# An attention-plus-wave-mixer kernel whose static order is planned anew: mixer weights earlier, batch 1 by head pair, two-chunk evictions, new issue times

## The chip, the cores and the metric

The kernel runs on one core of a Trainium2 chip. The metric is device time in microseconds (us), the median of several executions. Executions of one kernel mostly agree within a per cent; a few fall in a slower state, told by a time over 1.5% above the fastest of the same kernel. Wherever I give a ratio, it is the mean time of one kernel's fast runs over that of the other kernel's fast runs of the same rounds, so it is not quite the ratio of the medians that stand beside it, which count the slow runs too.

The engines: PE is TensorE (PEld its weight loads), DVE is VectorE, ACT is ScalarE, POOL is GpSimd, SP is SyncE, which here does nothing but issue DMAs. In these traces each engine works off its own instructions in the emitted order: further down, VectorE stands idle for 2.82 us before a cast while work behind it has its data. That is what this case is about.

## The reference, cut to what matters

Eight batches, eight heads, 576 positions, head size 64. Linear attention (q times the 64x64 matrix k-transposed v), a root-mean-square norm, then a mixer over 512 channels:

```python
kv = np.einsum('bhsd,bhse->bhde', k, v)
out = np.einsum('bhsd,bhde->bhse', q, kv)
x = out / np.sqrt(np.mean(out * out, -1, keepdims=True) + 1e-6) * g_norm   # then heads side by side: [b, 576, 512]
theta = x @ w_theta
zr, zi = x * np.cos(theta), x * np.sin(theta)
y = einsum('ts,bsd->btd', w_tok_r, zr) + einsum('ts,bsd->btd', w_tok_i, zi)
u = x + y
return u + np.maximum(u @ w_ch, 0)
```

## The kernel before

The source does not fix the order of the instructions. It registers tasks (a load, a cast, a group of matmuls), each with an estimated cost on the engines that may do it, a due time, and what it needs. A planner, run when the kernel is built, simulates engines and DMA with these estimates and emits each task when its simulated turn comes. The emitted order is final: on the chip, an engine whose next instruction lacks its data stands still, even when a later instruction could run.

The planner's picture of the DMA is a single server. Of its loop (cuts marked by ...):

```python
RATE = 0.335e6          # bytes per us
BACKLOG = 3.5
...
if dma is not None:
    (first, size, packed) = dma
    begin = max(start + first, dma_free)
    dma_free = begin + size / self.RATE / packed
    end = dma_free + 0.35
done[name] = end
```

The q of batches 2 and later is cast to f16 on VectorE and turned by five transposing DMAs:

```python
nc.sync.dma_start_transpose(
    out=st["qT", b][:, :, j * P:j * P + rows],
    in_=qcast[b % 2][:rows, j].rearrange("p h d -> p (h d)"),
)
weave.add(("qT", b, j), [SP], due("turn_q", b, j), fn, ..., dma=dma(128e3, 0.24))
```

The last 64 rows of each batch are stored in two issues (`parts` are two halves of the partitions):

```python
for (half, r) in parts:
    nc.sync.dma_start(out=out[b, SF:S, r * n:(r + 1) * n], in_=t[half])
```

The token mix makes one matrix y per chunk of 128 channels and half of the positions, evicted as `uT = y * gcol + xT` by VectorE. At the start, "warm" matmuls on unused data fill TensorE's time.

## Time and profile before

The time before was 231.53 us (231.21 to 233.05); the profiled span is 230.3 us.

| | before |
|---|---|
| useful TensorE work, at the spacing of undisturbed stretches | about 194 us |
| first token-mix product y of batch 0 starts | 44.3 us |
| mixer weights issued | 23 to 33 us |
| last y products end, span ends | 222.2, 230.3 us |

Three views of the kernel before follow. First, from the page: the busy tenths of TensorE in 40 slices of the span, the granted clock of TensorE in tenths, the busy share of the DMA engines, and the chain of work that ended last.

```profile
PE   7999999999996999999999999999999999999992
PEclk9999999999999999999999999999999999999999
DMA  5899999999749996974899467996894412103214
PE 73%; DMA 9%; DVE 6%; ACT 5%; POOL 3%; issue 1%; SPq 1%; DVEq 0%
```

TensorE is busy from slice 1 to the end with one dip near 70 us, and three quarters of the chain is TensorE. DMA fills the first half of the span and thins out after three quarters.

Second, the median time from issue to landing of the large loads (tile, queue, kind and count, size, us).

```profile
q<-in_q_dram SPq DMA_DIRECT2D x32, 256.0 KB, 5.1
k<-in_k_dram SPq DMA_DIRECT2D x28, 256.0 KB, 5.1
v<-in_v_dram SPq DMA_DIRECT2D x28, 256.0 KB, 5.5
```

### The profile page before, as it was taken

The page shows a single profiled execution, that of the slowest core. Times are in us where ns is not written, and L with a number is a line of the kernel's source. Part 1 is how long each engine was busy: PE and PEld are TensorE (multiplying, and loading weights), DVE is VectorE, ACT ScalarE, POOL GpSimd, SP SyncE. Part 2 cuts the span into 40 slices and gives each one's busy share as a digit, 9 for nine tenths or more (in the row PEclk, how much of TensorE's full clock was granted, in tenths as well). Part 3 has the DMA queues.
Part 4 walks back from the last instruction along what each step waited for, and adds up shares of the span by engine and source line. Part 5 has one row for each costly group of instructions (what it writes and reads, how often), then busy time and mean ns, then how long its engine had stood idle before and what let it go on. Part 6 is the DMA issues. An engine that isn't in the chain of part 4 may idle for free.

```text
span 230.3 us, 5955 instructions
## 1 busy us (share of the span) xinstructions
PE 220.8 (96%) x2342; PEld 145.8 (63%) x2342; DVE 185.2 (80%) x368; ACT 157.3 (68%) x298; POOL 88.0 (38%) x108
## 2 busy tenths in 40 slices
PE   7999999999996999999999999999999999999992
PEld 2674555786754665677667766865675668655861
DVE  2268599279997798799999997998799989987553
ACT  2477687327995688767896877589849797877031
POOL 8000197436513670464266033543275336430000
PEclk9999999999999999999999999999999999999999
DMA  5899999999749996974899467996894412103214
GB/s 184 291 344 239 291 254 313 330 272 335 127 124 260 340 162 159 331 235 82 190 317 353 90 151 213 318 195 155 234 306 122 117 57 93 48 23 137 71 46 159
DMA packets 59931, 46.42 MB, mean 202 GB/s; under 512 B 29056, under 2 KB 52608, under 8 KB 59904
## 3 DMA queue, kind: packets, MB, share of 16 engines
q1 hardware_dynamic: 59840, 46.05, 71.9%
q8 instruction: 18, 0.29, 0.6%
q14 instruction: 9, 0.07, 0.1%
q0 software_dynamic: 64, 0.00, 0.0%
HBM read 33.06 MB, written 9.44 MB: 185 GB/s over the span
## 4 chain that ended last, share of the span: by engine, by line
PE 73%; DMA 9%; DVE 6%; ACT 5%; POOL 3%; issue 1%; SPq 1%; DVEq 0%
PE y L893 27%; PE vps L937 11%; PE th L806 11%; PE kv L524 6%; DMA wst<-in_moe_w_theta_dram 4%; PE xTps L775 4%; PE ups L928 4%; PE warm L293 3%; DMA vl<-in_v_dram 3%; PE raw L572 3%; DMA v<-in_v_dram 2%; POOL rt L594 2%; ACT tr L849 2%; DVE x L606 2%; PE wTps L432 2%; PE th L811 1%
## 5 line engine op out<-in xcount | busy, mean ns | idle before, releaser
L893 PE MATMUL y<-wT,z 128*128 128x320 f16 (+1 forms) x576 | 79.1, 286 | 2.2 <-DVE z L859 2.2
L893 PEld LDWEIGHTS <-z 128*128 128x128 f16 x576 | 54.0, 98 | 19.1 <-DVE z L859 2.8
L594 POOL TENSOR_TENSOR rt<-ss,mhalf 128x8 f32<-128x8 f32 x35 | 61.0, 1744 | 2.9
L590 POOL TENSOR_SCALAR ss<-ss 128x8 f32<-128x8 f32 x35 | 9.5, 271 | 85.2 <-DVE ss L583 84.6
L901 DVE SCALAR_TENSOR_TENSOR uT<-y,gcol,xT 128x256 f16<-128x256 f32 (+1 forms) x64 | 32.7, 512 | 7.9 <-PE y L893 7.6
L937 PE MATMUL vps<-wch,uT 128*128 128x512 f16 (+1 forms) x192 | 37.7, 344 | 0.0
L818 ACT ACTIVATE pt<-th,magic_t 128x512 f32<-128x512 f32 (+1 forms) x40 | 25.7, 642 | 16.6 <-PE th L806 13.3
L806 PE MATMUL th<-wth,xT 128*128 128x512 f16 x128 | 32.7, 380 | 0.0
L784 ACT ACTIVATE xT<-xTps,gcol 128x512 f16<-128x512 f16 (+1 forms) x36 | 22.9, 635 | 13.3 <-PE xTps L775 13.0
L944 ACT COPY u<-ups 128x512 f16<-128x512 f16 (+1 forms) x40 | 21.0, 537 | 14.9 <-PE ups L928 14.6
L859 DVE TENSOR_TENSOR z<-x,tr 128x1024 f16<-128x1024 f16 (+1 forms) x40 | 27.0, 674 | 3.4 <-ACT tr L849 1.7
L948 DVE SCALAR_TENSOR_TENSOR ot<-vps,u 128x512 f32<-128x512 f32 (+1 forms) x40 | 25.2, 633 | 4.1 <-PE vps L937 2.6
L822 DVE SCALAR_TENSOR_TENSOR f<-pt,th 128x512 f32<-128x512 f32 (+1 forms) x40 | 25.2, 629 | 4.0 <-ACT pt L818 3.7
L606 DVE TENSOR_TENSOR x<-raw,rt 128x512 f16<-128x512 f32 x36 | 24.7, 685 | 3.0 <-POOL rt L594 2.4
L583 DVE TENSOR_REDUCE ss<-sq 128x8 f32<-128x512 f32 x36 | 24.3, 680 | 2.3 <-ACT sq L579 2.0
L293 PE MATMUL warm<-kvbd 128*128 128x512 f16 x81 | 23.4, 410 | 2.0 <-DVE pio_t L250 1.5
L841 ACT ACTIVATE tr<-fa,pio_t 128x512 f16<-128x512 f32 x32 | 23.0, 720 | 0.5 <-DVE fa L829 0.3
L841 ACT ACTIVATE tr<-f 128x512 f16<-128x512 f32 x32 | 20.2, 630 | 3.4 <-DVE f L822 3.2
L579 ACT ACTIVATE sq<-raw 128x512 f32<-128x512 f32 x36 | 21.1, 591 | 1.2 <-PE raw L572 0.9
L937 PEld LDWEIGHTS <-uT 128*128 128x128 f16 (+1 forms) x192 | 14.1, 102 | 8.1 <-issue 0.4
L524 PE MATMUL kv<-v,k 128*64 128x64 f32 x448 | 19.0, 227 | 0.0
L524 PEld LDWEIGHTS kv<-v,k 128*64 128x64 f32 x448 | 15.3, 137 | 5.6 <-issue 4.2
(80 smaller groups left out, 243.4 us busy)
## 6 DMA issues: line engine op xcount, KB each, us to landing
q<-in_q_dram SPq DMA_DIRECT2D x32, 256.0 KB, 5.1
out_dram<-ot SPq DMA_DIRECT2D x32, 256.0 KB, 3.6
k<-in_k_dram SPq DMA_DIRECT2D x28, 256.0 KB, 5.1
v<-in_v_dram SPq DMA_DIRECT2D x28, 256.0 KB, 5.5
k<-in_k_dram SPq DMA_DIRECT2D x4, 288.0 KB, 6.2
v<-in_v_dram SPq DMA_DIRECT2D x4, 288.0 KB, 6.4
wmix<-in_moe_w_tok_r_dram SPq DMA_DIRECT2D x4, 288.0 KB, 5.5
wmix<-in_moe_w_tok_i_dram SPq DMA_DIRECT2D x4, 288.0 KB, 4.0
```

Of the source, the lines that this page charges most:

```text
L293: nc.tensor.matmul(t[:], kv_bd[1][:, 0, :], kv_bd[1][:].rearrange("p h c -> p (h c)"), start=True, stop=True,)
L524: nc.tensor.matmul(kvp[r * D:(r + 1) * D, hp, :], st["k", b, hp][:, r, j, :] if j < NF else st["kl", b][:, 2 * hp + r, :], st["v", b, hp][ ...
L594: nc.gpsimd.tensor_tensor(out=r[:], in0=t[:], in1=mhalf[:], op=ALU.pow)
L606: nc.vector.tensor_tensor(out=t[:].rearrange("p (h e) -> p h e", h=H), in0=st[raw][:].rearrange("p (h e) -> p h e", h=H), in1=st[rt][:].un ...
L806: nc.tensor.matmul(t[:], xT[:, kc, :], wth[:, kc, :], start=(kc == 0), stop=(kc == NK - 1),)
L818: nc.scalar.activation(out=t[:], in_=st[th][:], func=AFT.Identity, bias=magic_t[:])
L822: nc.vector.scalar_tensor_tensor(out=t[:], in0=st[pt][:], scalar=MAGIC, in1=st[th][:], op0=ALU.subtract, op1=ALU.subtract,)
L841: nc.scalar.activation(out=t[:, which, :], in_=src[:], func=AFT.Sin, scale=-RAD, bias=0.0 if bias is None else bias[:],)
L859: nc.vector.tensor_tensor(out=t[:], in0=xb.unsqueeze(1).broadcast_to((P, w, C)), in1=st[tr][:, 0:w, :], op=ALU.mult,)
L893: nc.tensor.matmul(t[:], z[:, kc * P:(kc + 1) * P], wT[m][:, cols], start=(m == 0), stop=(m == NM - 1),)
L901: nc.vector.scalar_tensor_tensor(out=st["uT", b][:, kc, cols], in0=st[y][:], scalar=gcol[:], in1=st["xT", b][:, kc, cols], op0=ALU.mult, o ...
L937: nc.tensor.matmul(t[half], uT(kc), wch[:, kc, r * n:(r + 1) * n], start=(kc == 0), stop=(kc == NK - 1),)
```

## The change

Its intent: shorten the start (get to y earlier), take some work off VectorE, and plan the order with a finer picture of SyncE, on which an issue now takes 0.4 to 1.3 us, where it took 0.1 before. Its core, with cuts; the due times, period, margins and the `MIX_AFTER`/`WCH_AFTER` places of the weights were all searched anew:

```diff
-    "load": (-15.33, 2.93),       # due times of the tasks, 17 entries
+    "load": (-20.73, 4.16),       # 21 entries, all changed
 ...
-MIX_AFTER = 5
-WCH_AFTER = 7
+MIX_AFTER = 3                     # mixer weights before batch 1's loads
+WCH_AFTER = 6
-    RATE = 0.335e6
-    BACKLOG = 3.5
+    LANES = 8
 ...
-                dma_free = begin + size / self.RATE / packed
-                end = dma_free + 0.35
+                dma_free = max(start + first, dma_free) + took
+                end = dma_free + 0.2
 ...
-    SP = ("SP", 0.1, 0.1)
+    def sp(cost):
+        return ("SP", cost, cost, False)
 ...                                # loads of 256 KB: 0.78 us before
-                      makes=[(kind, f"{kind}{b}_{hp}")], dma=dma(size, 1.0), load=True)
+                      makes=[(kind, f"{kind}{b}_{hp}")], dma=dma(0.71), load=True)
 ...                                # transposing DMAs of q
-            weave.add(("qT", b, j), [SP], ..., dma=dma(128e3, 0.24))
+            weave.add(("qT", b, j), [sp(1.3)], ..., dma=dma(0.5))
 ...                                # g_norm as a row, turned by a matmul with sqrt(D)
-                nc.gpsimd.dma_start(out=gcol[r * D:(r + 1) * D, :], in_=g_norm.unsqueeze(1))
+                nc.gpsimd.dma_start(out=grow[:, r * D:(r + 1) * D], in_=g_norm.unsqueeze(0))
 ...                                # batch 1 goes through the head-pair path of batch 0
-            if b == 0:
-                first(hp)
-                continue
-            if b == 1:
-                turn_q_by_pe(b, hp)
-            attention(b, hp)
+            if b < 2:
+                by_pair(b, hp)
+            else:
+                attention(b, hp)
 ...                                # mix: half 0 in banks of two chunks
-        (half, kc) = divmod(i, NK)
+        half = int(i >= NK // 2)
+        kcs = [i - NK // 2] if half else [2 * i, 2 * i + 1]
 ...                                # last 64 rows of a batch in one store
-            for (half, r) in parts:
-                nc.sync.dma_start(out=out[b, SF:S, r * n:(r + 1) * n], in_=t[half])
+            nc.sync.dma_start(
+                out=out[b, SF:S, :].rearrange("t (r c) -> r t c", r=len(parts)), in_=t[:]
+            )
```

In batch 0 half 0's sums are also left open, so that y accumulates as the z tiles appear; and the casts of the weights may go to VectorE and ScalarE as well as GpSimd.

## The prediction

> **What bounds it now.** The page gives PE busy 220.8 of 230.3 us, but 81 matmuls of that are idle work ("warm"): start to start in the timeline they cover 21.5 us, before 45 us. Useful matmuls (as many after) at their usual spacing (0.216 us per 128x512, 0.136 per 128x320, 0.109 per 128x256, 0.73 per 20 kv) sum to about 194 us. So PE is the limit from 44 us on (chain of waits: mostly y, vps, th); the start is what can be saved. There the timeline shows: theta begins at 25.2 us; mixer weights are issued only from 23 us, after two head pairs of batch 1; GpSimd casts them from 28.2 to 38.6; the last turned wT is kept near 43.9; the first y starts at 44.3 although the last z of batch 0 ended at 39.3. Another 3 us go at 68.7 to 71.9: y of batch 1 waits for DVE z.
>
> **What the change does.**
> - Mixer loads move straight behind theta (program order): 1.8 MB of batch 1 no longer precede them, 6 us at the page's 300 GB/s. DVE and ACT share the casts.
> - Half 0 of batch 0's mix accumulates as z tiles appear, and batch 1's attention goes by head pair: PE has real work while it waits (54 warm instead of 81).
> - Half 0 evictions: 32 of 128x256 (477 ns, 0.4 spacing) become 16 of 512 columns (about 0.6): 3 us less DVE in all, little each; DVE is not the later limit (about 20.5 us per batch against 22-23 on PE).
> - The Sin table load (1.28 us; the Trainium skill, "ScalarE: Activation LUTs", What ACT_TABLE_LOAD costs, has 1283 ns) sits at 22.05 before the last xT of batch 0; moved behind: theta 1 us earlier.
> - g_norm: gcol is ready at 13.7 now, first used at 14.6: worth nothing.
> - Last store in one issue: -0.5 us.
>
> **Cost.** At the start DVE now limits. From the first f (about 26.3 us) its new order up to batch 0's last uT adds up, at measured spacings, to 24.4 us: done at about 51 instead of 62. In the order, 163.5 us of useful PE work remain from batch 0's last y product, which then starts near 49.5. Add 3 to 6 us of stalls (3 us after 96 us in this trace) and 4.4 us of tail: 220.5 to 223.5 us span; the reported time was 1.2 us above the span. DVE or ACT, in order, may stand behind a late cast: up to 2 us more. GpSimd casts beside z stretched it to 1.0-1.3 us (mean 0.74) at 30-38 us, as the Trainium skill's "SBUF — State Buffer", Who interferes with whom, says for tensor_tensor with two SBUF inputs; casts now end by about 30.
>
> **Predicted:** 222.8 us, 8 in 10 between 219 and 228. Faster by over 2%: 0.87; within 2%: 0.11; slower: 0.02.
>
> **What would show it.** Right: mixer DMAs issued from 13-20 us; casts over by 31; first y about 35, last uT of batch 0 near 51; first y of batch 1 near 64 (now 68.4, really 71.9), no DVE z wait; batch spacing unchanged at about 23 us.
>
> **What would make it wrong.** DVE or ACT stalled on late casts; batch 1's later loads starving its head pairs; "mm" banks held longer by two-chunk y, so PE waits for evictions; the serial pow on GpSimd (1.7 us, five for batch 1) delaying batch 1's x.

## More of the kernel before

Third, the waits of VectorE for q (total us, times, longest).

```profile
DVE qcast L453 <- DMA q<-in_q_dram: 4.9, 2, 2.7
DVE qcast L459 <- DMA ql<-in_q_dram: 1.9, 1, 1.9
```

They are few, and all three lie in the first 26 us. The order of this kernel fits the arrival of its data.

## The result, and the profile after

The changed kernel took **249.2 us** (246.45 to 250.63, 4 runs), the kernel before 232.04 us in the same rounds. Two of the four runs are slow; the fast ones took 246.45 and 248.21 us, so between fast runs the loss is about 15 us, not the 17 us between the medians. The ratio of the fast runs is 1.066 (95% interval 1.055 to 1.076): slower by 6.6%, where I had given "slower" two chances in a hundred. The profiled run is a fast one; its span is 244.7 us.

The same views of the changed kernel. First the page's slices and chain.

```profile
PE   7899989989849888977999989699999999999980
PEclk9999999999988999997999999999999999999998
DMA  6998999999999979969989895936221013015023
PE 39%; DMA 23%; DVE 14%; ACT 9%; SPq 6%; POOL 4%; issue 2%; POOLq 1%; ACTq 0%
```

TensorE has holes up to about 160 us; the chain is 39% TensorE and 23% DMA, where it was 73% and 9%. DMA is full until about 155 us and nearly idle after: with the same bytes, this order asks for its data earlier.

Then the time from issue to landing.

```profile
q<-in_q_dram SPq DMA_DIRECT2D x32, 256.0 KB, 6.1
k<-in_k_dram SPq DMA_DIRECT2D x28, 256.0 KB, 7.2
v<-in_v_dram SPq DMA_DIRECT2D x28, 256.0 KB, 6.9
```

And the waits. VectorE now waits ten times for q and four times for ql, 21 us in all, far into the kernel; TensorE waits for v and for VectorE.

```profile
DVE qcast L479 <- DMA q<-in_q_dram: 15.3, 10, 2.8
DVE qcast L485 <- DMA ql<-in_q_dram: 6.0, 4, 2.4
PE raw L569 <- DVE x L603: 5.2, 3, 2.1
PE kv L521 <- DMA v<-in_v_dram: 3.3, 1, 3.3
```

**The start went much as predicted.** Mixer weights were issued from 12.9 to 22.6 us, GpSimd's casts ended at 28.0 (38.6 before), the first y started at 36.3 (predicted 35; 44.3 before). Then the gain was lost:

| first y of batch | 0 | 1 | 2 | 3 | 4 | 5 | 6 | 7 |
|---|---|---|---|---|---|---|---|---|
| before, us | 44.3 | 68.4 | 96.2 | 123.1 | 143.7 | 165.6 | 189.8 | 212.1 |
| after, us | 36.3 | 72.1 | 102.8 | 131.3 | 151.8 | 178.2 | 202.3 | 223.1 |

**The first standstill, line by line.** In the timeline of SyncE of the changed kernel (start, duration, both in us), five transposing DMAs of batch 2 hold the queue for 8 us, and only then comes the next q load.

```profile
56.62 7.99 SPq L503 DMA_TRANSPOSE qT<-qcast  x5
64.65 0.58 SPq L329 DMA_DIRECT2D q<-in_q_dram  x1
65.79 0.47 SPq L329 DMA_DIRECT2D v<-in_v_dram  x1
```

In the timeline of VectorE, the cast of that q stands next in the order; VectorE is idle for 2.82 us before it (in brackets), though work behind it had its data (the last input of the z at 68.16 was done at 64.6). It happens again at the next cast.

```profile
67.62 0.43 DVE L479 CAST qcast<-q 128x512 f16<-128x512 f32 x1 [2.82 <-DMA q<-in_q_dram]
68.16 0.68 DVE L892 TENSOR_TENSOR z<-xp,tr 128x1024 f16<-128x1024 f16 x1
71.97 0.43 DVE L479 CAST qcast<-q 128x512 f16<-128x512 f32 x1 [2.52 <-DMA q<-in_q_dram]
```

TensorE meanwhile stands at a product that needs the v of the same head pair, and y of batch 1 waits behind it.

```profile
71.37 0.69 PE L521 MATMUL kv<-v,k 128*64 128x64 f32 x16 [3.33 <-DMA v<-in_v_dram]
72.11 5.12 PE L935 MATMUL y<-wT,z 128*128 128x256 f16 x30
```

How fast the DMA moved data around the transposes is in a table by stretches. Its columns: stretch, length, busy us of PE, PEld, DVE, ACT and POOL (with instruction counts), granted clock, DMA share, GB/s. Changed kernel first:

```profile
48.00:56.60 8.60, 7.92 (x63) 4.84 (x63) 6.71 (x15) 3.91 (x7) 3.81 (x4) 1.00 1.15 308
56.60:64.60 8.00, 7.31 (x111) 4.53 (x109) 6.97 (x15) 7.16 (x14) 0.00 (x0) 1.00 1.29 125
71.30:80.00 8.70, 8.17 (x73) 6.33 (x73) 5.25 (x11) 1.28 (x2) 3.81 (x4) 0.80 1.11 321
```

And the kernel before, at its own transposes of batch 2:

```profile
49.00:57.00 8.00, 8.00 (x80) 5.25 (x78) 7.23 (x16) 3.96 (x8) 5.54 (x6) 1.00 1.03 337
57.00:65.50 8.50, 8.50 (x113) 5.58 (x111) 8.42 (x17) 7.89 (x15) 4.10 (x5) 1.00 0.67 130
```

In both kernels the DMA moves 308 to 337 GB/s before the transposes and 125 to 130 GB/s while they run. The Trainium skill, "Advanced Engine Details and Errata", X-Bar Transpose (TRN2), says that transposing DMAs on this chip "are as fast as regular DMAs". In this trace they are not: five of them, 0.6 MB, take 8.0 us. The measurement decides. What they use up is SyncE's queue: one holds it for 1.39 us on average (30 in the changed kernel, 1.18 to 2.34), a load of 256 KB for 0.47 us in the median, and SyncE issues nothing else meanwhile. That they also slow transfers beside them is not shown: in the changed kernel the rate was down to 139 to 159 GB/s from 55.0 us on, before the first of them was issued, while the kl, vl and ql loads moved in rows of 256 bytes. The old plan gave a transpose 0.1 us of SyncE and 1.59 us of DMA, 8 us for five; the new one gave it 1.3 us of SyncE and 0.5 us of DMA.

The last of the stretches shows a second loss: after TensorE's idle 3.3 us its granted clock averages 0.80 over 8.7 us. The Trainium skill, "TensorE: Matmul & The Clock Gate", What's actually happening, says that the clock falls to half after an idle window of about 3.4 us and comes back after about as long a busy one. The trace agrees: 3.4 us at half speed in 8.7 us would average 0.80 (an estimate from that page's figure), and its clock record has half speed from 72.2 to 75.6 us.

**Plan against trace.** The planner's own times can be printed when the kernel is built and set against the trace, task by task. This was the most useful table. It shows how much later than planned the first uT of each batch, and the last VectorE task of all, ended:

| | plan's end of VectorE work | lag at batch 0 | 1 | 2 | 3 | 4 | 6 | end |
|---|---|---|---|---|---|---|---|---|
| before | 221.3 | 5.3 | 5.3 | 5.4 | 5.3 | 6.0 | 6.0 | 5.4 |
| after | 214.6 | 5.6 | 12.1 | 17.9 | 20.8 | 24.9 | 24.5 | 24.1 |

The plan of before is off by a constant: it is a true plan. The plan of after promised 6.7 us less, and fell behind by 18.5 us more, in steps that stand at late q, ql and v, between 50 and 155 us, until the loads are done.

### The profile page after: what moved, and what is told of

Its sections match the earlier page's. It is cut to its first block, busy times and chain, and to the rows that moved or that the text cites. A ratio compares the mean times of both kernels' runs of the same rounds, so it can differ in the third digit from the quotient of the medians.

```text
span 244.7 us, 5897 instructions
## 1 busy us (share of the span) xinstructions
PE 219.7 (90%) x2317; PEld 147.3 (60%) x2317; DVE 183.3 (75%) x367; ACT 157.4 (64%) x302; POOL 81.3 (33%) x97
## 4 chain that ended last, share of the span: by engine, by line
PE 39%; DMA 23%; DVE 14%; ACT 9%; SPq 6%; POOL 4%; issue 2%; POOLq 1%; ACTq 0%
DMA q<-in_q_dram 14%; PE y L935 14%; PE vps L993 6%; PE th L839 4%; DMA ql<-in_q_dram 4%; PE kv L521 3%; DMA grow<-in_g_norm_dram 3%; DVE ss L580 3%; DMA vl<-in_v_dram 3%; SPq L329 2%; DVE x L603 2%; SPq L503 2%; ACT tr L882 2%; PE warm L315 2%; DVE uT L946 2%
## 5 line engine op out<-in xcount | busy, mean ns | idle before, releaser
L935 PE MATMUL y<-wT,z 128*128 128x320 f16 (+1 forms) x576 | 80.8, 293 | 1.4 <-DVE ot L1004 1.3
L935 PEld LDWEIGHTS <-z 128*128 128x128 f16 x576 | 55.6, 100 | 17.9 <-issue 2.5
L591 POOL TENSOR_TENSOR rt<-ss,mhalf 128x8 f32<-128x8 f32 x31 | 52.6, 1698 | 2.6
L946 DVE SCALAR_TENSOR_TENSOR uT<-y,gcol,xT 128x320 f16<-128x320 f32 (+1 forms) x48 | 29.1, 610 | 7.3 <-PE y L935 7.3
L1004 DVE SCALAR_TENSOR_TENSOR ot<-vps,u 128x512 f32<-128x512 f32 (+1 forms) x40 | 25.1, 632 | 6.5 <-DMA out_dram<-ot 2.2
L576 ACT ACTIVATE sq<-raw 128x512 f32<-128x512 f32 x32 | 18.6, 595 | 15.8 <-PE raw L569 15.6
L855 DVE SCALAR_TENSOR_TENSOR f<-pt,th 128x512 f32<-128x512 f32 (+1 forms) x40 | 24.9, 624 | 1.5 <-ACT pt L851 1.3
L479 DVE CAST qcast<-q 128x512 f16<-128x512 f32 x32 | 13.6, 424 | 15.3 <-DMA q<-in_q_dram 15.3
L603 DVE TENSOR_TENSOR x<-raw,rt 128x512 f16<-128x512 f32 x32 | 21.8, 683 | 3.6 <-POOL rt L591 3.5
L580 DVE TENSOR_REDUCE ss<-sq 128x8 f32<-128x512 f32 x32 | 21.3, 677 | 1.2 <-ACT sq L576 1.0
L892 DVE TENSOR_TENSOR z<-x,tr 128x1024 f16<-128x1024 f16 (+1 forms) x32 | 19.7, 616 | 1.6 <-ACT tr L874 1.0
L795 ACT ACTIVATE xT<-xTps,gcol 128x512 f16<-128x512 f16 (+1 forms) x32 | 20.1, 630 | 0.8 <-PE xTps L786 0.6
```

The source lines that it names most:

```text
L580: nc.vector.reduce_sum(out=t[:], in_=st[sq][:].rearrange("p (h e) -> p h e", h=H), axis=mybir.AxisListType.X,)
L591: nc.gpsimd.tensor_tensor(out=r[:], in0=t[:], in1=mhalf[:], op=ALU.pow)
L603: nc.vector.tensor_tensor(out=t[:].rearrange("p (h e) -> p h e", h=H), in0=st[raw][:].rearrange("p (h e) -> p h e", h=H), in1=st[rt][:].un ...
L855: nc.vector.scalar_tensor_tensor(out=t[:], in0=st[pt][:], scalar=MAGIC, in1=st[th][:], op0=ALU.subtract, op1=ALU.subtract,)
L935: nc.tensor.matmul(st[y][:, c, :], z[:, kc * P:(kc + 1) * P], wT[m][:, cols], start=(c == 0 and m == 0) if open_sums else m == 0, stop=m = ...
L946: nc.vector.scalar_tensor_tensor(out=st["uT", b][:, chunks, cols], in0=st[y][:], scalar=gcol[:], in1=st["xT", b][:, chunks, cols], op0=ALU ...
```

## The experiments

My theory A: the order was planned with hopeful DMA figures; in-order engines then stand where the plan believed that the data was there. Rivals: the new work (two-chunk banks, head pairs, the g_norm row) is itself slower; or the order merely asks too early; or single casts are misplaced. All experiments gave correct results. Lag means the table's measure.

### Putting the DMA figures of before into the new plan: all, only transposes, only loads and stores

```diff
 # e1_turns: the changed kernel, one number
-                      dma=dma(0.5))
+                      dma=dma(1.59))
 # e1_loads: the changed kernel, the others
-dma=dma(0.71)   # load       +dma=dma(0.78)
-dma=dma(0.9)    # tail       +dma=dma(0.87)
-dma(0.66 .. 0.8)  # weights  +dma(0.78 .. 0.88)
-dma(0.65 .. 0.4)  # stores   +dma(0.87 .. 0.44)
-end = dma_free + 0.2         +end = dma_free + 0.35
 # e1_all: both
```

> The changed kernel, with only the planner's DMA figures set back to those of the kernel before (load of 256 KB 0.78 us instead of 0.71, each DMA transpose 1.59 instead of 0.5, store 0.87 instead of 0.65, 0.35 instead of 0.2 after the last byte). Theory A (the new plan counts on data that has not landed, so in-order DVE stands at the q casts): DVE waits for q loads after 30 us fall from 21 us to under 4, DVE runs at a constant lag behind its plan (5 to 7 us), time 230 to 235 us. Rival B (the new structure itself, two-chunk banks and batch 1 by head pair, or plain DMA bandwidth): still 242 us or more.

> The changed kernel, with only the DMA time that the planner gives each transpose of q set back from 0.5 to 1.59 us. Theory A1 (it is the transposes that the plan underrates): nearly all of the loss goes, 226 to 231 us. Theory A2 (it is the rate of the plain loads and stores): little changes, over 240 us. Rival B: over 242 us.

> The changed kernel, with only the planner's figures for loads and stores set back (0.78 and 0.87 us, 0.35 us latency), transposes left at 0.5. Theory A2: 226 to 231 us. Theory A1: over 238 us, with waits for q just behind each block of transposes. Rival B: over 242 us.

Measured: e1_all 238.36 us (ratio to before 1.023, interval 1.018 to 1.027), e1_turns 238.31 us (1.025, 1.021 to 1.028), e1_loads 249.62 us (1.072, 1.067 to 1.077). So the transposes' figure alone brings back about 9.5 of the 15 us between fast runs (ratio 1.025 against 1.066), and the other figures nothing. Both kernels that got it missed my numbers: I had expected 226 to 235 us. The lag of e1_turns goes from 5.0 to 11.8 us instead of staying level, so something else was still late.

### The reverse: hopeful figures in the plan of before

```diff
 # b_fast: the kernel before, all of the change's DMA figures
-    RATE = 0.335e6
+    RATE = 0.369e6
-                end = dma_free + 0.35
+                end = dma_free + 0.2
-                      dma=dma(128e3, 0.24))
+                      dma=dma(0.5 * Weave.RATE, 1.0))
-                  uses=[ot], dma=dma(n * P * 4, 0.9))
+                  uses=[ot], dma=dma(n * P * 4, 1.09))
 # b_turn: the kernel before, the transposes' figure alone (1.59 us becomes 0.5)
-                      dma=dma(128e3, 0.24))
+                      dma=dma(128e3, 0.764))
```

> The kernel before, with only the planner's DMA figures made as hopeful as the changed kernel's (0.71 us per 256 KB, 0.5 per transpose, 0.65 per store, 0.2 after). Its plan then ends 3.6 us earlier. Theory A: the chip is slower, not faster: 236 to 245 us, with DVE waits for q after 45 us. Rival B: 227 to 232 us, as before or a little better.

> The kernel before, with one number of its planner changed: a transposing DMA of 128 rows is planned at 0.5 us instead of 1.59 us; loads, stores and the rest stay as they were. Its own plan ends at 220.2 us of DVE work instead of 221.4. Theory A (the changed kernel loses its time because its order was planned with transposing DMAs three times too short): most of the 24 us that all hopeful DMA figures cost this kernel come back with this one number, 242 to 256 us, VectorE waiting 15 us or more in all for q and ql loads. Rival (the loads and stores planned too short do it, or only both together): at most 237 us, those waits under 8 us.

Measured: b_fast 256.21 us (1.102, 1.095 to 1.109); b_turn 252.86 us (1.081, 1.074 to 1.088), against 232.0 to 232.5 for the kernel before. In b_turn one number that no instruction contains, only the planner's belief about a transposing DMA, costs 8%: the instructions are the same (the two traces hold the same ones on every engine, line by line) and only their order differs. Its plan ended 1.1 us *earlier* than that of before (220.2); in the trace the lag climbs from 4.7 us at batch 0 to 29. The waits of b_turn, whose profiled run is one of its two slow ones:

```profile
DVE qcast L459 <- DMA ql<-in_q_dram: 18.1, 6, 5.4
DVE qcast L453 <- DMA q<-in_q_dram: 7.8, 6, 3.3
PE kv L524 <- DMA v<-in_v_dram: 4.8, 2, 4.5
```

These are the same waits as in the changed kernel, with none of the changed work. So this number alone is enough for such a loss, and e1_turns shows that it is the larger part of it in the changed kernel.

Where the lag arises can be read on SyncE's queue, each DMA's planned issue against the trace. In b_turn the lag of the queue jumps by 4.4 to 5.8 us in each of the six blocks of transposes, 30 us in all (b_fast, profiled in a fast run: 28.8 us); in the kernel before it changes by -1.5 to +0.4 us. The changed kernel is different, since it plans 1.3 us of SyncE for a transpose: of the 16.4 us by which the lag of its queue grows from the first block to the last (8.7 to 25.1 us), only 4.8 arise in the blocks (1.5 in the first, shown above) and the rest between them. There the number presumably acts through the order, by how soon after a block the plan puts the tasks that need the loads behind it; that is my reading and not isolated. Nor is it settled whether the missing time belongs to SyncE or to the DMA: the fits below put 1.87 and 1.95 us of a transpose on SyncE's queue, and 0.34 and 0.84 us on the DMA.

### Is it only a few casts, or only asking too early?

```diff
 # a_qlate: the changed kernel; its planner takes q and ql of batches 2 and later to land 4.5 us later
 # a_hold: the changed kernel; its planner holds back the casts and k-v products of batch b
-                  needs=[("q", b, hp)], makes=first,
+                  needs=[("q", b, hp)] + ([("uT", b - 2, 0)] if b > 1 else []), makes=first,
 ...               # the same for the ql cast, and ("uT", b - 2, hp) for the k-v product
```

> The changed kernel, whose plan counts q and the last rows of q of batches 2 to 7 as landing 4.5 us later; k, v, the order and pace of the DMA issues are planned with the same figures as in the change. It moves DVE's q casts (and the transposes that need them) behind other work. Theory A, with DVE's in-order q casts as the place where the late data does its harm: most of the loss goes, 233 to 239 us, DVE waits for q after 45 us under 8 us (21 in the changed kernel). If the harm is done at the k and v loads in front of TensorE, or by the pace of the DMA itself: over 243 us.

> The changed kernel with its hopeful DMA figures kept, but its planner may not cast q of batch b, or multiply its k and v, before uT tiles of batch b-2 are done. In the plan the last q cast then leads the first y of its batch by 37 to 43 us (batches 3 to 7), as in the kernel before (37 to 43), instead of 46 to 62 in the changed kernel; the plan ends at 220.0 instead of 214.6 us. Theory L (the order asks for the next batch's data too early, and that lead is all that is wrong): 226 to 234 us, waits of VectorE for q under 6 us. Rival T (wherever a transposing DMA and the loads behind it stand, the plan takes them for landed some us too soon, and the engines stand there in order): 240 to 252 us, with waits for DMAs of 12 us or more.

Measured: a_qlate 245.51 us (1.059, 1.052 to 1.067), a miss: the waits for q fell to 8.9 us and those for ql to 2.4, but others took their place (VectorE's last stage for its output buffers 3.9 us, TensorE for turned q 2.3 and for v 2.4), and the lag still rose from 8.5 to 21 us. The casts are only where late data shows first. a_hold: 251.15 us (1.083, 1.074 to 1.091), so theory L falls: with the cast leading y by as much as in the kernel before, nothing came back; VectorE now waited 12.4 us for output buffers. Where the order asks is not the fault by itself; the plan puts wrong things side by side as long as it believes the transposes short.

### The parts of the change by themselves

```diff
 # a_col: the changed kernel with g_norm fetched as a column again
 # b_row: the kernel before with g_norm as a row, turned by a matmul
 # b_two: the kernel before with half 0 of the mix in two-chunk banks
```

> The changed kernel with g_norm fetched as a column of 128 one-element rows and scaled by DVE, as before; its planned time is left as in the change. If the row lands earlier, as the change intends, DVE's wait before gcol grows from 0.9 us by a microsecond or more. My reading: both forms land 6 to 6.5 us after the issue, so the first batch is no later than with the row (gcol within 1 us of 12.2 us), and the time stays within 2% of the changed kernel's, 244 to 252 us.

> The kernel before with only the row fetch of g_norm and the TensorE turn, planned with the old 9 us. Worth nothing by itself: 230 to 234 us; gcol ready within 1 us of 13.7 us.

> The kernel before with only the two-chunk banks of token mix half 0 (no open sums). If two-chunk banks make TensorE wait for evictions (a rival cause of the loss): over 236 us and DVE waits on y grow. Theory A: 229 to 235 us, DVE busy about 3 us less (16 evictions of 512 columns for 32 of 256), no new TensorE wait on DVE uT.

Measured: b_row 232.75 us (1.002, 0.996 to 1.008): worth nothing, as predicted. a_col 249.9 us (1.077, 1.070 to 1.084), no better than the changed kernel, nor clearly worse (that one's interval is 1.055 to 1.076). The form of the fetch does not decide when it lands: a row lands 6.5 to 6.8 us after issue in the changed kernel and 5.4 to 5.5 in b_row, a column 6.1 to 6.2 before and 5.7 to 6.2 in a_col; the new plan counts 5.0. b_two 234.99 us (1.011, 1.007 to 1.016): VectorE is busy 181.6 us instead of 185.2, so the two-chunk evictions save the predicted 3 us, yet the time is not shorter, since VectorE is not the limit; the new order had a 3.8 us hole of TensorE that ends at 73.4 us. Alone, none of these parts costs anything like 15 us, or gains. The head pairs of batch 1 and the earlier mixer weights were not tried alone; that they do not make the loss follows only from e2_turns_st and tuned_c below, which have them and lose nothing.

### The changed work with a plan that fits the chip

tuned_a and tuned_b are the changed kernel with its planner's DMA figures fitted to the twelve traces that I had by then, and the due times, margins and lanes searched for these figures.

```diff
 # tuned_b, besides the due times, margins, lanes and other loads and stores
+DMA = {"load": 0.82, "tail": 0.65, "weight": 0.93, "turn": 0.84, "store": 0.68, "first": 1.25, "after": 0.38, "issue": 1.95}
-            weave.add(("qT", b, j), [sp(1.3)], ..., dma=dma(0.5))
+            weave.add(("qT", b, j), [sp(DMA["issue"])], ..., dma=dma(DMA["turn"]))
-        weave.add("grow", [("POOL", 1.3, 5.0, False)], -100.0, fetch)
+GROW = 10.5
+        weave.add("grow", [("POOL", 1.3, GROW, False)], -100.0, fetch)
```

> The changed kernel's work with another plan: the planner's DMA figures are fitted to the twelve traces (a 256 KB load 0.81 us, a transposing DMA 1.87 us on the SyncE queue instead of 1.3, the g_norm row landing after 10.5 us instead of 5.0), and its due times, margins and lanes are searched anew for these figures. Its plan of DVE work ends at 220.6 us. If wrong DMA figures are what spoilt the changed kernel, its work planned with right ones should show a lag between plan and trace that stays within 3 us from the first batch to the last, waits of VectorE for q and ql under 5 us, and 224 to 229 us, which beats both kernels. Rival (the changed work itself is slower, whatever the plan): 234 us or more.

> As tuned_a, from another start of the search, nearer to the changed kernel's order (mixers before batch 1's loads, 56 idle matmuls at the start): load 0.82 us, transposing DMA 1.95 us on the queue and 0.84 us of DMA. Its plan of DVE work ends at 219.3 us. Expected as for tuned_a: 224 to 229 us with a steady lag if the figures were the fault; 234 us or more if the changed work is slower whatever the plan.

Measured: tuned_a 236.25 us (1.016, 1.012 to 1.021), tuned_b 234.51 us (1.008, 1.004 to 1.013). The lag of tuned_b stays between 4.5 and 7.9 us, so the plan is nearly true again, and about 13 of the 15 us between fast runs are back. But both miss my 224 to 229 us. Looking for the rest I saw that VectorE ends as early in tuned_b as in the kernel before (226.6 and 226.7 us), but the spans end at 232.4 and 230.3.

### The last store

The stretches after the last VectorE instruction (ends 238.8) of the changed kernel, in the columns of before:

```profile
239.30:240.30 1.00, 0.00 (x0) 0.00 (x0) 0.00 (x0) 0.00 (x0) 0.00 (x0) 1.00 0.71 258
240.30:241.30 1.00, 0.00 (x0) 0.00 (x0) 0.00 (x0) 0.00 (x0) 0.00 (x0) 1.00 0.13 39
242.30:243.30 1.00, 0.00 (x0) 0.00 (x0) 0.00 (x0) 0.00 (x0) 0.00 (x0) 0.77 0.13 47
```

And of the kernel before (last VectorE instruction ends at 226.7):

```profile
227.20:228.20 1.00, 0.00 (x0) 0.00 (x0) 0.00 (x0) 0.00 (x0) 0.00 (x0) 1.00 0.84 286
228.20:229.20 1.00, 0.00 (x0) 0.00 (x0) 0.00 (x0) 0.00 (x0) 0.00 (x0) 1.00 0.27 67
```

The one-issue store trickles at 37 to 47 GB/s with a DMA share of 0.13, which is two engines of 16. The Trainium skill, "DMA: Bandwidth & Descriptors", Why a DMA increments its semaphore by 16 and not by 1, gives the reason: such a DMA is spread over the largest number of engines, at most 16, that divides the slowest dimension on both sides. The rearranged output has a slowest dimension of 2; the two stores before have 64 rows each. The trace agrees. The span ended 5.8 to 5.9 us after the last VectorE instruction in every trace with the one-issue store, and 3.6 us after it in those with two. Whether it also held up loads in the middle was open, and with it whether the new work could win. Four more kernels:

```diff
 # a_two_st, e2_turns_st, tuned_c: the changed kernel, e1_turns and tuned_b with
-            nc.sync.dma_start(
-                out=out[b, SF:S, :].rearrange("t (r c) -> r t c", r=len(parts)), in_=t[:]
-            )
+            for (half, r) in parts:
+                nc.sync.dma_start(out=out[b, SF:S, r * n:(r + 1) * n], in_=t[half])
 # b_one_st: the reverse, in the kernel before
```

> The changed kernel with only its last store of each batch issued as two stores of 64 rows, as in the kernel before; plan and order stay the same. In the trace of the changed kernel the one-issue store moved 128 KB at about 47 GB/s with a DMA share of 0.13 (two of 16 engines), and the span ended 5.9 us after the last VectorE instruction, against 3.6 before. Theory E (it costs only at the end): 2.2 us faster than the changed kernel, about 247 us, waits for q and ql as before. Theory M (in the middle too it holds up the loads that share its two engines, and is a main cause): at most 242 us, waits of VectorE for q and ql at least 6 us fewer than 21.

> The kernel before with only the last store of each batch in one issue, as the change does. Theory E: 2.2 us slower than before, all of it after the last VectorE instruction (5.9 instead of 3.6 us). Theory M: 4 us or more slower, with a lag that grows in the middle.

> The changed kernel with transposing DMAs planned at 1.59 us (238.3 us measured) and two stores for the last tile of each batch. Theory E: 236 us. Theory M: at most 233 us.

> tuned_b (234.5 us) with two stores for the last tile of each batch. Theory E: 232.3 us, level with the kernel before. Theory M: at most 230 us, faster than before.

| kernel | median us | ratio to before (interval) | without this edit |
|---|---|---|---|
| b_one_st | 234.46 | 1.009 (1.005 to 1.013) | 1 |
| a_two_st | 246.16 | 1.058 (1.054 to 1.062) | 1.066 (1.055 to 1.076) |
| e2_turns_st | 233.44 | 1.002 (0.998 to 1.006) | 1.025 (1.021 to 1.028) |
| tuned_c | 229.89 | 0.990 (0.986 to 0.993) | 1.008 (1.004 to 1.013) |

In the kernel before, the one-issue store costs 2.2 us, all of it at the end (its lag stays at 3.9 to 5.0): theory E. In a_two_st the gain is about 2 us too, but the two intervals overlap. In e2_turns_st and tuned_c it is 4 to 5 us: more than the tail, less than I had expected of theory M for e2_turns_st. The lag of tuned_c is 3.1 to 5.1 us where that of tuned_b was 4.5 to 7.9, so there the one-issue stores seem to hold up other work before the end as well. That they do so through the transfers on their two engines is seen in the lag at most, not isolated.

tuned_c beats both kernels: 229.9 us against 232.2 and 249.2. It is 1% faster than the kernel before, clear of the noise. Of tuned_c, the busy times and the waits for q:

```profile
PE 215.6 (95%) x2319; PEld 145.5 (64%) x2319; DVE 185.9 (82%) x378; ACT 156.1 (69%) x300; POOL 76.4 (34%) x88
DVE qcast L481 <- DMA q<-in_q_dram: 4.6, 3, 2.0
DVE qcast L487 <- DMA ql<-in_q_dram: 1.4, 2, 1.1
```

The waits are those of the kernel before again (4.9 and 1.9 us), and TensorE is busy 95% of a span of 227.3 us. The gain at the start shrinks to 3 us of span: its first y of batches 0 to 4 start at 35.6, 67.2, 92.8, 118.5 and 140.6 us, so 8.7 us ahead of before at the start, 1.2 at batch 1, and 3 to 5 from batch 2 on.

## Why the prediction was wrong, point by point

- **Right: the start.** Mixer weights issued from 12.9 to 22.6 us (predicted 13 to 20), casts over by 28.0 (by 31), first y at 36.3 (about 35), 54 warm matmuls; the last y product of batch 0 started at 52.1 where I had 49.5, and its last uT ended at 55.4 where I had 51, in part because batch 1's casts and copies stand between. The whole z tiles of batch 0 take 0.68 us each after the casts on GpSimd are gone, where they took 1.0 to 1.3 beside them: so what the Trainium skill, "SBUF — State Buffer", Who interferes with whom, was cited for in the prediction is seen in both traces.
- **Right: small terms.** The g_norm row was worth nothing (b_row, a_col). The two-chunk evictions saved 3.6 us of VectorE in b_two, and little of the time.
- **Wrong, the step that failed:** "163.5 us of useful PE work remain from batch 0's last y product ... Add 3 to 6 us of stalls (3 us after 96 us in this trace)". I took the stalls of the old trace over to a new order. From the last y product of batch 0 to the last matmul the changed kernel took 185.8 us (52.1 to 237.9), so stalls and slower clock came to 22.3 us instead of 3 to 6, as I counted the useful work. TensorE's idle time between 45 and 195 us, read from the stretches of 25 us, was 14.7 us against 3.1 before. The clock ran at half speed from 72.2 to 75.6 and from 113.1 to 116.5 us (0.93 in two of those stretches), which costs about 3.4 us more; some 4 us of the 22.3 stay unexplained. I had read in the diff that all DMA figures of the planner changed, and did not ask whether they agreed with the trace that I had: the five transposes stood there, 8 us long, in front of me, and the new plan gave them 1.3 us of SyncE and 0.5 us of DMA each. b_turn shows that the 0.5 alone costs the kernel before about 19 us between fast runs, and e1_turns that it is worth 9.5 of the 15 us here.
- **Capped too low:** "DVE or ACT, in order, may stand behind a late cast: up to 2 us more." The mechanism was named, with the wrong size. VectorE stood 21.3 us at q and ql casts (6.8 before). And "batch 1's later loads starving its head pairs" was near, but it was the loads of batch 3 and later, behind the transposes.
- **Wrong sign:** "Last store in one issue: -0.5 us." It costs 2.2 us at the end (b_one_st). I counted issues, and did not look at what the new shape does to the number of engines.
- **Not held, or not shown:** "Batch spacing unchanged at about 23 us" did not hold: from first y to first y it was 35.8, 30.7, 28.5, 20.5, 26.4, 24.1 and 20.8 us. The first y of batch 1 came at 72.1 us where I had 64; TensorE had stood 3.33 us for a v just before it. And since the due times were all searched together, how much of the changed kernel's loss lies in the due times by themselves was not separated. e2_turns_st, with the transposes' figure and the store mended and every due time as the change has it, is level with before, so they cost little more than the gain at the start.

The sum of the misses against my 222 us of span: 2.6 us at the start, 16 to 19 us of stalls and clock beyond the 3 to 6, and 2.4 us after the last matmul (6.8 instead of 4.4); together the 22.7 us that the span of 244.7 exceeded it.

## What to carry to other kernels

When a kernel's order comes from a planner, its cost figures are part of the kernel: set each changed figure against the trace before believing the order, and set the plan's times against the trace task by task; a lag that stayed constant was harmless here, and one that grew in steps showed where data came late. In these kernels optimism about a transpose was dear (8% in b_turn) and pessimism cheap (tuned_c counts 1.95 us of SyncE for what takes 1.37 on average, and is the fastest): a load planned too early stops the engine that waits for it, everything behind it, and then the clock. Before merging two stores into one, look at the slowest dimension of the merged pattern: here it became 2, and two of 16 DMA engines worked.

## What the Trainium skill lacked or had wrong

- "Advanced Engine Details and Errata", X-Bar Transpose (TRN2), has transposing DMAs as fast as regular ones. Here five of them (0.6 MB from SBUF to SBUF, f16) held SyncE's queue for 8.0 us, 1.25 to 2.3 us each, where a load of 256 KB holds it for 0.47 us; in those 8.0 us all DMA traffic together was 125 GB/s. What they do to loads already under way no run here shows.
- No page says how much a static order loses when a planned DMA time is too short: here 8% for one figure (b_turn, ratio 1.081).
